# Other byte offsets for weights, h and turned output, and a later place for the split of the turned output

## The chip, the cores and the metric

The kernel runs on one core of one Trainium2 chip. The metric is the device time of one execution in microseconds (us). A profile of one execution gives, for each engine, what ran when and what it waited for. The engines are PE (TensorE, matrix products; the loads of its stationary operand are listed as PEld), ACT (ScalarE), DVE (VectorE), POOL (GpSimd) and SP (the engine that issues most of the transfers). Working memory (SBUF) has 128 partitions; a byte offset in this text is the offset within one partition. Products land in the PSUM banks.

## What is computed

With x of 2048 rows and 576 columns, everything in float32:

```
xn  = layernorm(x)
q, k, v = split(xn @ wqkv)            # 32 heads of 18 columns
logits[s, w] = q[s] . k[s - 2 w] / sqrt(18),  w = 0..7   (masked where s - 2 w < 0)
o   = sum_w softmax(logits)[s, w] * v[s - 2 w]
h   = relu(xn @ w1)                   # 4608 columns
out = x + o @ wo + h @ w2
```

## The kernel before

**Precision.** PE multiplies in the type float32r. Each operand that needs the full precision is split into a high part (ACT copies it to float32r) and a low part (DVE subtracts the high part from the raw value). A product is then three: high by high, high by low, low by high. `hi_lo` (L278) makes such a pair of operations.

**Work and order.** The 2048 rows are handled in two phases (`NPH`) of 1024 rows (8 row tiles, each of 128 rows). In a phase there are 18 blocks `n` of 256 columns of w1, and for each block two halves `h` of 512 rows; such a pair is a group `g`, 72 in all. A group makes h for its block (first layer, x moving and a *weight set* `wset` stationary, 256 columns at a time), splits h into `hhi` and `hlo`, and multiplies them by `w2t` (second layer, `o_step`, L720: h stationary, w2 moving in pieces of 256 and 320 columns; six matmuls, three products by two pieces, make one step, and a step writes the accumulator `po`). Most groups form the first layer by seven products of sums (`pstep`, L605, called P1 to P7) in place of eight plain ones (`classic`, L583). For one block in about four, q, k and v of a quarter of the heads are made too (`qkv_tile`, L778; x stationary, 432 columns of wqkv moving, 14 matmuls, 8 tiles per quarter and phase, 64 in all), and the attention of that quarter follows on DVE (`attention`, L818).

**The turned output.** The output of attention must be stationary for the product with wo, so it has to be turned. DVE turns it in blocks of 32 by 32 (`turn`, L881), SP stores it to DRAM as `turned` (L891), and `wo_h` (L666) loads it back in column order into `olo` (L681, or L685 for the 16 leftover columns of each quarter), lets ACT copy the high part to `ohi` and lets DVE subtract to leave the low part in `olo`. Steps of kind "wo" in `o_step` then use `ohi` and `olo` as stationary operands, with `v` (a buffer of the pool vp, here holding wo, split by `wo_make`, L519) moving.

**What sets the order.** The program is written out by a planner (`Order`, L53). PE's order is given by the loops. ACT and DVE each have a list of waiting operations; an operation becomes ready when the planner thinks its predecessors have ended, and among the ready ones the one with the earliest due time goes first. Work of attention on DVE goes into a background list (`later`) that fills the gaps. A transfer (`send`, L151) is issued on SP in the order of the calls; its assumed landing time is worked out from its size, and a `margin` can be added to it (L160):

```
        op.end = max(start + 2.1, self.dma + 1.2) + margin
```

On the chip each engine runs its instructions in the written order and each waits for its own semaphores. The margin is thus not a wait; it only changes where the planner places what depends on the transfer.

**Where tiles lie.** Tiles lie one behind the other, in the order of the pools and, within `keep`, of the calls. `keep` holds x (`X`), its split and summed forms (`XA`, `XS`, `XR`), the two weight sets (`BUF`; set 0 for even blocks, set 1 for odd ones, and for wqkv in the block before), k (`KK`), `TS`, q/o (`QO`) and two sums. Then come `w2p` (w2), `hp` (h), `whp` (the turned output), `vp` (v and wo), and the rest.

Of the kernel before, what the change touches and what calls it, by code (L numbers as in the profile page):

```python
# [16 lines left out]
P = 128  # L17
# [11 lines left out]
WOP = ((6, 9, 13, 16), (7, 10, 14, 17))  # L29
HALO = ((0, 112), (112, 127))  # L30
WARM = 24

S2, S4, S3, S1 = range(4)
T1, B11, T2, B21, T3, B22, T4, RR = range(8)
# [155 lines left out]
def tile_body(ctx: ExitStack, tc: tile.TileContext, x, wqkv, wo, w1, w2, out):  # L190
# [14 lines left out]
    ctx.enter_context(tc.manual_schedule())  # L205
    pool = lambda name, bufs, **k: ctx.enter_context(tc.tile_pool(name=name, bufs=bufs, **k))
    keep = pool("keep", 1)
    w2p = pool("w2p", 4)
    hp = pool("hp", 5)
    whp = pool("whp", 2)  # L210
    vp = pool("vp", 2)
    prp = pool("prp", 2)
    lgp = pool("lgp", 1)
    smp = pool("smp", 2)
    mvp = pool("mvp", 8)
    dram = pool("dram", 1, space=bass.MemoryType.DRAM)
    psp = pool("psp", 1, space=PSUM)

# [11 lines left out]
    XA = [[keep.tile([P, 2, KT, TBN], F32R, name=f"xa{h}{j}") for j in range(2)] for h in range(2)]  # L230
    XS = [keep.tile([P, 2, 4, 2, TBN], F32R, name=f"xs{h}") for h in range(2)]
    XR = [keep.tile([P, 3, TBN], F32R, name=f"xr{h}") for h in range(2)]
    BUF = [keep.tile([P, 10 * 3 * UD], F32R, name=f"wset{b}") for b in range(2)]
    KK = keep.tile([P, W - 1 + NI, UD], F32, name="kk")
    TS = keep.tile([P, 4, 2, P], F32, name="ts")
    VV = {}
# [7 lines left out]
    bk3 = psp.tile([P, 512], F32, name="bk3")  # L244
    pm = psp.tile([P, 512], F32, name="pm")

    def wset(m):
        z = BUF[m % 2].rearrange("p (e c) -> p e c", e=2)[:, :, 0:2048]
        return z.rearrange("p e (s k c) -> p e s k c", s=8, k=2)

    def wqset(p):
        return BUF[(p + 1) % 2].rearrange("p (t c) -> p t c", t=10)

    def raw_view(z):
        v = z.rearrange("p w c -> p (w c)")[:, 0 : 8 * TBN].rearrange("p (j s k c) -> p j s k c", j=2, s=2, k=2)
        return [v[:, 0], v[:, 1]]
# [18 lines left out]
    def mm(o, l, r, start, stop):  # L275
        nc.tensor.matmul(o, l, r, start=start, stop=stop, skip_group_check=True)  # L276

    def hi_lo(hi, lo, raw, n, after, slack):  # L278

        a = act(lambda: copy(hi, raw), n, after, slack)  # L280
        b = dve(lambda: sub(lo, raw, f32(hi)), n, [a], slack + 0.8)
        return [a, b]
# [215 lines left out]
    def wq_make(p, u, kts, raw=None):  # L498

        w = wqset(p)  # L500
        b = (p + 1) % 2
        v = wqkv.rearrange("r (s c) -> r s c", s=3)[:, :, u * UD : (u + 1) * UD] if raw is not None else WQC[u]
        for kt in kts:
            z = raw[:, kt] if raw is not None else f32(w)[:, 5 + kt]
            after = [] if raw is not None else [kept["wq", u]]
            free = slots_free(b, range(432 * kt // 256, min(7, (432 * kt + 431) // 256) + 1))
            if raw is None:
                after += free
            z3 = z.rearrange("p (s c) -> p s c", s=3)
            if kt < KT:  # L510
                g = [send(lambda: nc.sync.dma_start(z3, v[kt * P : (kt + 1) * P]), 221, after)]
            else:
                g = [send(lambda rows=rows: nc.sync.dma_start(z3[rows], v[KT * P : D]), 110, after)
                     for rows in (slice(0, DR), slice(DR, P))]
            WQOK.setdefault(p, []).extend(hi_lo(w[:, kt], w[:, 5 + kt], z, 3 * UD, [*g, *free], 2.5))

    WO, WOOK = {}, {}

# [147 lines left out]
    def wo_h(g, u, j):  # L666
        ph, n, h = G[g]
        i = 4 * h + 2 * j
        if g == NG - 1:
            z = w2p.tile([P, 2, D], F32R, name="w2t")  # L670
            ni = 4
            hi, lo = z[:, 0, 0 : ni * P], z[:, 1, 0 : ni * P]
            for q in range(2):
                WOH[g, u, q] = hi[:, q * TBN : (q + 1) * TBN], lo[:, q * TBN : (q + 1) * TBN]
        else:
            ni = 2
            hi, lo = whp.tile([P, TBN], F32R, name="ohi"), whp.tile([P, TBN], F32R, name="olo")
            WOH[g, u, j] = hi, lo
        v = lambda z: z.rearrange("p (i c) -> p i c", i=ni)
        if u < NU:  # L680
            s = [send(lambda: nc.sync.dma_start(v(f32(lo)), OT[u, i : i + ni].rearrange("i c k -> c i k")), 128, turned[ph, u])]  # L681
            low = lambda: sub(lo, f32(lo), f32(hi))
        else:
            s = [
                send(lambda rows=rows: nc.sync.dma_start(v(f32(lo)[rows]), OTR[i : i + ni].rearrange("i c k -> c i k")), 64, turned[ph, u])  # L685
                for rows in (slice(0, DR), slice(DR, P))
            ]
            low = lambda: sub(hi[DR:P], f32(lo[DR:P]), f32(hi[DR:P]))
        a = act(lambda: copy(hi, f32(lo)), ni * P, s, 4)
# [88 lines left out]
    def qkv_tile(p, u, i):  # L778
        ph = p // NP
        if i == 0:  # L780
            o_.force(KFREE[0])
            VV[u % 2] = vp.tile([P, W - 1 + NI, UD], F32, name="v")
            nc.gpsimd.memset(KK[0:1, 0 : W - 1, :], 0.0)
            nc.gpsimd.memset(VV[u % 2][0:1, 0 : W - 1, :], 0.0)
        k, v, q = KK, VV[u % 2], QO[u % 2]
        h, j, c = place(i)
        xa, wq = XA[h][j], wqset(p)
        o = pm[:, 0 : 3 * UD]
        lst = (
            [(xa[:, 0, kt, c], kt) for kt in range(KT)] + [(xa[:, 1, kt, c], kt) for kt in range(KT)]  # L790
            + [(XR[h][:, j, c], 4)] + [(xa[:, 0, kt, c], 5 + kt) for kt in range(KT)] + [(XR[h][:, j, c], 9)]
        )

        def f():
            for z, (l, b) in enumerate(lst):
                mm(o, l, wq[:, b], z == 0, z == len(lst) - 1)

        t = pe(f, 14 * 0.196, [*WQOK[p], *XOK[h, j], *BANK["pm"]])
        pq = o.rearrange("p (s c) -> p s c", s=3)

        def out_():
            copy(k[:, W - 1 + i, :], pq[:, 1])
            copy(v[:, W - 1 + i, :], pq[:, 2])
            copy(q[:, i, :], pq[:, 0])

        e = act(out_, 3 * (UD + 70), [t, *OFREE[u % 2]], 1.2)
        BANK["pm"] = [e]
        SETFREE[(p + 1) % 2] = {q: t for q in range(8)}
# [9 lines left out]
    def attention(ph, u, halo):  # L818
# [4 lines left out]

        def begin():
            s["lg"] = lgp.tile([P, NI, W, HG], F32, name="lg")
            s["m"] = smp.tile([P, NI, HG], F32, name="m")
            s["r"] = smp.tile([P, NI, HG], F32, name="r")

        def spread(z):
            return z[:, :, None, :].to_broadcast([P, NI, W, HG])  # L830
# [208 lines left out]
        RAWR.pop(h, None)  # L1039

    def x_home(h):
        KR[h] = raw_view(vp.tile([P, W - 1 + NI, UD], F32, name="v") if h else KK)

    for h in range(2):
        g = GP - 1 + h
# [32 lines left out]

    x_first(0)
    x_first(1, nc.scalar)  # L1080
    VV[0] = vp.tile([P, W - 1 + NI, UD], F32, name="v")
    ST0 = VV[0].rearrange("p w c -> p (w c)")[:, 0:1280].rearrange("p (s k c) -> p s k c", s=5, k=2)
    RAWS = ((B11, 0, 0), (B21, 256, 0), (RR, 512, 0), (B12, 0, 1), (B22, 256, 1))
    SETOK[0] = {}
# [24 lines left out]

    KFREE[0] = WQOK[0]  # L1110
    OFREE[0] = [*W2OK[0, 0], *W2OK[0, 1]]
    KR[0] = raw_view(vp.tile([P, W - 1 + NI, UD], F32, name="v"))
# [127 lines left out]
```

## Time and profile before

| | |
|---|---|
| median of 3 runs | 1200.48 us (1198.25 to 1200.82) |
| the profiled execution | 1201.66 us |
| its span, first to last instruction | 1199.9 us |
| granted TensorE clock, mean | 0.990 |
| DMA, mean | 96 GB/s |

The profile comes as a page (busy shares, slices, DMA, the chain, the costliest groups, the transfers), and its trace answers further questions. In rows of groups, `out<-in` names what is written and read, then come partitions and elements, the count, the busy time in us with the mean of one in ns, and behind the second bar the idle time before, with what ended it. A matmul's duration overlaps the next one's, so the pace is the distance of the starts, not the duration. The chain is the work that ended last, followed back from the end. Rows of waits read "engine, line, waited for, engine, line: us in total, times, longest us". Rows of the timeline and of the chain begin with the start and the length in us.

### The profile page before, as it was taken

Reading aid. Unit: us, or ns where it says so; the run is one execution under the profiler, and the core shown is the slowest. Engines: PE = TensorE matmul, PEld = TensorE weight load, DVE = VectorE, ACT = ScalarE, POOL = GpSimd, SP = SyncE. Lnnn points to the kernel's source line nnn. Section 1 sums busy time; section 2 is a strip of 40 time slices with the busy share of each in tenths; the row PEclk is TensorE's granted clock in tenths of the full one; section 3 lists DMA queues with packets and bytes.
Section 4 is the critical chain, followed back from the end, with each engine's and each line's share of the span. In section 5 each row is a group of like instructions: output and inputs, shape, how many; then the busy total and the mean of one; then the engine's idle time right before and its main releaser. Section 6 shows DMA issues by size and latency. Waiting matters only on the chain.

```text
span 1199.9 us, 21930 instructions
## 1 busy us (share of the span) xinstructions
PE 1162.5 (97%) x8528; PEld 1140.0 (95%) x8528; DVE 826.4 (69%) x1533; ACT 743.0 (62%) x1658; POOL 64.2 (5%) x97
## 2 busy tenths in 40 slices
PE   7999999999988999999999999999999999999998
PEld 6899999999988999899999999999999999999998
DVE  7648978953988169774683299589925994399731
ACT  5548466655656466566686567476646665566663
POOL 2200200110011001000010000000000000000000
PEclk8999999999999999899999999999999999999999
DMA  6752441562245232333352222231322213221322
GB/s 197 218 139 69 150 106 56 161 170 84 68 148 158 42 92 83 120 78 88 120 173 93 71 66 58 44 103 44 89 54 85 71 52 72 83 59 56 80 66 89
DMA packets 133544, 115.60 MB, mean 96 GB/s; under 512 B 54128, under 2 KB 112240, under 8 KB 133120
## 3 DMA queue, kind: packets, MB, share of 16 engines
q1 hardware_dynamic: 128192, 85.00, 25.7%
q0 software_dynamic: 5104, 28.90, 7.5%
q8 instruction: 67, 1.10, 0.4%
q14 instruction: 37, 0.30, 0.1%
q10 hardware_dynamic: 144, 0.29, 0.1%
HBM read 96.01 MB, written 36.50 MB: 110 GB/s over the span
## 4 chain that ended last, share of the span: by engine, by line
PE 73%; DVE 12%; ACT 8%; issue 3%; DMA 3%; POOL 0%; SPq 0%; ACTq 0%; DVEq 0%; POOLq 0%
PE po L276 32%; PE bk L276 21%; PE pm L276 14%; PE bkA L276 5%; DVE wset L273 3%; ACT po L270 2%; ACT x L270 2%; DVE ts L273 2%; DMA olo<-turned 1%; DVE hlo L554 1%; ACT wset L270 1%; DVE sn L273 1%; ACT hhi L270 1%; DVE pr L870 1%; DVE pr L840 1%
## 5 line engine op out<-in xcount | busy, mean ns | idle before, releaser
L276 PE MATMUL po<-w2t,hhi 128*128 128x256 f32 (+1 forms) x2304 | 407.1, 299 | 6.1 <-ACT po L270 5.9
L276 PEld LDWEIGHTS po<-w2t,hhi 128*128 128x128 f32 x2304 | 341.0, 190 | 10.9 <-ACT po L270 9.7
L276 PE MATMUL po<-w2t,hlo 128*128 128x256 f32 (+1 forms) x1152 | 248.1, 297 | 0.0
L276 PE MATMUL bk<-xs,wset 128*128 128x256 f32 x1632 | 238.2, 282 | 7.0 <-DVE sn L273 7.0
L270 ACT ACTIVATE x<-po 128x576 f32<-128x576 f32 x286 | 182.2, 644 | 100.3 <-PE po L276 97.6
L276 PEld LDWEIGHTS bk<-xs,wset 128*128 128x128 f32 x1632 | 217.7, 189 | 8.1 <-DVE sn L273 7.8
L276 PEld LDWEIGHTS po<-w2t,hlo 128*128 128x128 f32 x1152 | 195.7, 191 | 0.0
L270 ACT ACTIVATE po<-x 128x576 f32<-128x576 f32 x286 | 187.0, 654 | 2.9
L276 PE MATMUL pm<-wset,xa 128*128 128x432 f32 x768 | 172.9, 360 | 2.6 <-ACT wset L270 1.5
L276 PEld LDWEIGHTS pm<-wset,xa 128*128 128x128 f32 x768 | 140.2, 188 | 9.9 <-ACT qo L270 2.3
L276 PE MATMUL bk<-xa,wset 128*128 128x256 f32 x924 | 138.7, 288 | 7.5 <-DVE hlo L554 4.8
L273 DVE TENSOR_TENSOR sn<-bk,sn 128x256 f32<-128x256 f32 x136 | 57.2, 421 | 122.0 <-PE bk L276 81.2
L276 PEld LDWEIGHTS bk<-xa,wset 128*128 128x128 f32 x924 | 125.8, 193 | 13.2 <-DVE hlo L554 10.1
L273 DVE TENSOR_TENSOR w2t<-w2t 128x576 fp32r<-128x576 f32 (+1 forms) x72 | 54.1, 751 | 70.1 <-ACT w2t L270 69.4
L270 ACT ACTIVATE hhi<-sn 128x256 fp32r<-128x256 f32 x136 | 56.4, 415 | 72.7 <-DVE sn L273 72.7
L270 ACT ACTIVATE kk<-pm 128x144 f32<-128x144 f32 (+1 forms) x68 | 21.0, 308 | 114.6 <-PE pm L276 114.4
L870 DVE TENSOR_TENSOR pr<-lg,v 128x1152 f32<-128x1152 f32 x64 | 85.1, 1352 | 0.2
L276 PE MATMUL bk<-xr,wset 128*128 128x256 f32 x426 | 85.1, 281 | 0.0
L840 DVE TENSOR_TENSOR pr<-qo,kk 128x1152 f32<-128x1152 f32 x64 | 85.0, 1351 | 0.0
L843 DVE TENSOR_REDUCE lg<-pr 128x64 f32<-128x1152 f32 x64 | 84.8, 1345 | 0.0
L273 DVE TENSOR_TENSOR wset<-wset 128x512 fp32r<-128x512 f32 (+2 forms) x120 | 70.8, 599 | 11.9 <-ACT wset L270 11.5
L276 PE MATMUL bkA<-xa,wset 128*128 128x256 f32 x480 | 68.9, 281 | 2.0 <-DVE xr L273 2.0
(132 smaller groups left out, 1365.5 us busy)
## 6 DMA issues: line engine op xcount, KB each, us to landing
w2t<-w2c SPq DMA_DIRECT2D x70, 288.0 KB, 2.8
wset<-w1c SPq DMA_DIRECT2D x106, 128.0 KB, 2.4
w1c<-in_w POOLq DMA_DIRECT2D x18, 576.0 KB, 8.4
w2c<-in_w POOLq DMA_DIRECT2D x18, 576.0 KB, 8.8
wset<-wqc SPq DMA_DIRECT2D x28, 216.0 KB, 2.5
out<-x SPq DMA_DIRECT2D x16, 288.0 KB, 2.2
wset<-w1c SPq DMA_DIRECT2D x70, 64.0 KB, 2.2
ts<-w1c SPq DMA_DIRECT2D x34, 128.0 KB, 2.7
```

The lines of the kernel that those rows point to most:

```text
L270: nc.scalar.activation(o, i, func)
L273: nc.vector.tensor_tensor(o, a, b, op=op)
L276: nc.tensor.matmul(o, l, r, start=start, stop=stop, skip_group_check=True)
L554: nc.vector.scalar_tensor_tensor(lo, src, 0.0, f32(hi), op0=ALU.max, op1=ALU.subtract)
L840: nc.vector.tensor_tensor(pr[i], q, window(k, i), op=ALU.mult)
L843: nc.vector.tensor_reduce(s["lg"][:, i], pr.pop(i).rearrange(heads, d=Dh), axis=AX.X, op=ALU.add)
L870: nc.vector.tensor_tensor(pr[i].rearrange(heads, d=Dh), e, window(v, i).rearrange(heads, d=Dh), op=ALU.mult)
```

## The change

It has two parts.

*Addresses.* Three pads are put between pools and one into `keep`. The weight sets get 2 x 2176 columns each in place of 4320, so that the high half and the low half lie a whole number of 256 bytes apart, and `wqset` takes five row blocks from either half. The buffers of vp get 2176 columns, too. To make room, the pool of small statistics goes from 8 to 6 buffers, and m and r of the softmax from 2 to 1. From the sizes follow the offsets modulo 256 bytes:

| tile | before | after |
|---|---|---|
| x forms xa, xs, xr | 192 | 192 |
| weight set 0, high and low half | 192, 128 | 0, 0 |
| weight set 1, high and low half | 64, 0 | 0, 0 |
| w2t, high and low half | 128, 128 | 0, 0 |
| hhi, hlo | 128 | 128 |
| ohi, olo | 128 | 128 |
| v / wo, its two buffers | 128, 64 | 0, 0 |
| kk | 192 | 0 |
| ts, qo, sn | 128 | 192 |

h and the turned output move by whole multiples of 256 bytes; against the operands that they are multiplied with, they change.

*Order.* The load of the turned output gets a margin of 2.5 us (1.5 us for the leftover columns), so the planner places the copy to `ohi` and the subtraction to `olo` behind other work. PE's order and POOL's order stay as they are. On ACT and DVE the copies and subtractions move by a few places, and other operations shift with them. On SP six loads of a weight set move behind the stores of the turned output and the load of the leftover columns, once near the end of each phase.

```
@@
+PADS = (16, 16, 32, 32)
@@
     keep = pool("keep", 1)
+    pad1 = pool("pad1", 1).tile([P, PADS[1]], F32, name="pad1")
     w2p = pool("w2p", 4)
+    pad2 = pool("pad2", 1).tile([P, PADS[2]], F32, name="pad2")
     hp = pool("hp", 5)
     whp = pool("whp", 2)
+    pad3 = pool("pad3", 1).tile([P, PADS[3]], F32, name="pad3")
     vp = pool("vp", 2)
...
-    mvp = pool("mvp", 8)
+    mvp = pool("mvp", 6)
@@
-    BUF = [keep.tile([P, 10 * 3 * UD], F32R, name=f"wset{b}") for b in range(2)]
+    keep.tile([P, PADS[0]], F32, name="pad0")
+    BUF = [keep.tile([P, 2, 2176], F32R, name=f"wset{b}") for b in range(2)]
@@
+    def v_tile():
+        return vp.tile([P, 2176], F32, name="v")[:, 0 : (W - 1 + NI) * UD].rearrange("p (w c) -> p w c", w=W - 1 + NI)
+
     def wset(m):
-        z = BUF[m % 2].rearrange("p (e c) -> p e c", e=2)[:, :, 0:2048]
+        z = BUF[m % 2][:, :, 0:2048]
         return z.rearrange("p e (s k c) -> p e s k c", s=8, k=2)
 
     def wqset(p):
-        return BUF[(p + 1) % 2].rearrange("p (t c) -> p t c", t=10)
+        return BUF[(p + 1) % 2][:, :, 0 : 5 * 3 * UD].rearrange("p e (t c) -> p e t c", t=5)
@@ wq_make
-            z = raw[:, kt] if raw is not None else f32(w)[:, 5 + kt]
+            z = raw[:, kt] if raw is not None else f32(w)[:, 1, kt]
...
-            WQOK.setdefault(p, []).extend(hi_lo(w[:, kt], w[:, 5 + kt], z, 3 * UD, [*g, *free], 2.5))
+            WQOK.setdefault(p, []).extend(hi_lo(w[:, 0, kt], w[:, 1, kt], z, 3 * UD, [*g, *free], 2.5))
@@ wo_h
-            s = [send(lambda: nc.sync.dma_start(v(f32(lo)), OT[u, i : i + ni].rearrange("i c k -> c i k")), 128, turned[ph, u])]
+            s = [send(lambda: nc.sync.dma_start(v(f32(lo)), OT[u, i : i + ni].rearrange("i c k -> c i k")), 128, turned[ph, u], 2.5)]
...
-                send(lambda rows=rows: nc.sync.dma_start(v(f32(lo)[rows]), OTR[i : i + ni].rearrange("i c k -> c i k")), 64, turned[ph, u])
+                send(lambda rows=rows: nc.sync.dma_start(v(f32(lo)[rows]), OTR[i : i + ni].rearrange("i c k -> c i k")), 64, turned[ph, u], 1.5)
@@ attention
-            s["m"] = smp.tile([P, NI, HG], F32, name="m")
-            s["r"] = smp.tile([P, NI, HG], F32, name="r")
+            s["m"] = smp.tile([P, NI, HG], F32, name="m", bufs=1)
+            s["r"] = smp.tile([P, NI, HG], F32, name="r", bufs=1)
```

`qkv_tile` takes its row blocks by two indices in place of one, and the other places that took a buffer named v from vp call `v_tile`; both do the same as before.

More of the change, by code (lines that the diff above doesn't have):

```diff
@@ L781, in qkv_tile @@
             o_.force(KFREE[0])
-            VV[u % 2] = vp.tile([P, W - 1 + NI, UD], F32, name="v")
+            VV[u % 2] = v_tile()
             nc.gpsimd.memset(KK[0:1, 0 : W - 1, :], 0.0)
@@ L789, in qkv_tile @@
         lst = (
-            [(xa[:, 0, kt, c], kt) for kt in range(KT)] + [(xa[:, 1, kt, c], kt) for kt in range(KT)]
-            + [(XR[h][:, j, c], 4)] + [(xa[:, 0, kt, c], 5 + kt) for kt in range(KT)] + [(XR[h][:, j, c], 9)]
+            [(xa[:, 0, kt, c], (0, kt)) for kt in range(KT)] + [(xa[:, 1, kt, c], (0, kt)) for kt in range(KT)]
+            + [(XR[h][:, j, c], (0, 4))] + [(xa[:, 0, kt, c], (1, kt)) for kt in range(KT)] + [(XR[h][:, j, c], (1, 4))]
         )
@@ L795, in f @@
             for z, (l, b) in enumerate(lst):
-                mm(o, l, wq[:, b], z == 0, z == len(lst) - 1)
+                mm(o, l, wq[:, b[0], b[1]], z == 0, z == len(lst) - 1)
         t = pe(f, 14 * 0.196, [*WQOK[p], *XOK[h, j], *BANK["pm"]])
@@ L1041, in x_home @@
     def x_home(h):
-        KR[h] = raw_view(vp.tile([P, W - 1 + NI, UD], F32, name="v") if h else KK)
+        KR[h] = raw_view(v_tile() if h else KK)
     for h in range(2):
@@ L1080, in tile_body @@
     x_first(1, nc.scalar)
-    VV[0] = vp.tile([P, W - 1 + NI, UD], F32, name="v")
+    VV[0] = v_tile()
     ST0 = VV[0].rearrange("p w c -> p (w c)")[:, 0:1280].rearrange("p (s k c) -> p s k c", s=5, k=2)
@@ L1111, in tile_body @@
     OFREE[0] = [*W2OK[0, 0], *W2OK[0, 1]]
-    KR[0] = raw_view(vp.tile([P, W - 1 + NI, UD], F32, name="v"))
+    KR[0] = raw_view(v_tile())
     KR[1] = [
```

## The prediction

> **What bounds the kernel now.** I read the page first: the busy shares, the chain, the groups.
>
> ```profile
> span 1199.9 us, 21930 instructions
> PE 1162.5 (97%) x8528; PEld 1140.0 (95%) x8528; DVE 826.4 (69%) x1533; ACT 743.0 (62%) x1658; POOL 64.2 (5%) x97
> PE 73%; DVE 12%; ACT 8%; issue 3%; DMA 3%; POOL 0%; SPq 0%; ACTq 0%; DVEq 0%; POOLq 0%
> ```
>
> TensorE is busy for 97% of the span and holds 73% of the chain that ends last. So two things can move the time: how fast 8528 matmuls follow one another, and the few microseconds in which PE waits. The change touches both: the addresses touch the first, the later split touches the second. Next came the groups with shapes kept apart, for the counts.
>
> ```profile
> L276 PE MATMUL po<-w2t,hhi 128*128 128x320 f32 x1152 | 335.1, 313 | 0.0
> L276 PE MATMUL bk<-xs,wset 128*128 128x256 f32 x1632 | 238.2, 282 | 7.0 <-DVE sn L273 7.0
> L276 PE MATMUL po<-w2t,hlo 128*128 128x320 f32 x576 | 179.8, 312 | 0.0
> L276 PE MATMUL bk<-xa,wset 128*128 128x256 f32 x924 | 138.7, 288 | 7.5 <-DVE hlo L554 4.8 <-ACT xa L270 2.0
> L276 PE MATMUL bkA<-xa,wset 128*128 128x256 f32 x480 | 68.9, 281 | 2.0 <-DVE xr L273 2.0
> ```
>
> The second layer (w2t moving, h stationary) is 1152 + 576 = 1728 pairs of one matmul of 256 and one of 320 columns. The first layer (x moving, a weight set stationary) is 1632 + 924 + 480 = 3036 matmuls of 256 columns, in sixes, beside the short rest rows. Matmuls overlap, so their pace is read from the starts of successive groups in the timeline.
>
> **The stalls that the later split aims at.** Of the waits in two windows, the olo transfer comes first in both, followed by DVE behind ACT, and then PE itself.
>
> ```profile
> ACT ohi L270 <- DMA olo<-turned: 5.5, 1, 5.5
> DVE olo L273 <- ACT ohi L270: 4.1, 1, 4.1
> PE bk L276 <- DVE sn L273: 2.7, 1, 2.7
> PEld po L276 <- ACT po L270: 0.7, 1, 0.7
> ```
>
> ```profile
> ACT ohi L270 <- DMA olo<-turned: 5.6, 1, 5.6
> DVE olo L273 <- ACT ohi L270: 4.2, 1, 4.2
> PE bk L276 <- DVE sn L273: 2.9, 1, 2.9
> ```
>
> The first fence is 340 to 370 us, the second 478 to 510 us. The chain says how 5.5 us of ACT become 2.7 us of PE:
>
> ```profile
> 342.93 8.22 DMA olo<-turned
> 351.17 0.42 ACT ohi L270
> 351.62 0.42 DVE olo L273
> ...
> 353.65 0.35 DVE sn L273
> ```
>
> The transfer of the turned output takes 8.22 us here, where the median for these transfers is 2.7 us:
>
> ```profile
> olo<-turned SPq DMA_DIRECT2D x30, 128.0 KB, 2.7
> ```
>
> ACT stands before its copy, DVE stands before the subtraction that needs the copy, and behind that subtraction in DVE's queue is the sum sn, which frees the bank that PE's next product writes.
>
> **What the 2.5 us do.** They are no wait on the chip: they are added to the landing time that the planner assumes, so only the written order changes. In the changed program ohi stands one place later on ACT at this spot (behind the first hhi<-sn), and olo stands behind sn on DVE, where before it stood ahead of it. So sn no longer waits for the transfer, and the 2.7 and 2.9 us of PE go: -5.6 us. What is late next is ACT: it still stops at ohi until 351.17, with the second hhi<-sn, an evacuation of po and a fresh seed of po behind it. PE waits for such a seed already (the 0.7 us row), and it now reaches that point sooner; I give back 0.6 us, about that row, over both places: **-5.0 us**. Bounds: nothing gained, if ACT's stop replaces DVE's in full; 7.0 us gained, if the 0.7 us and as much at the second place go too. The four instructions that overtake cost nothing; ohi and olo get later by about 1 us and are first used ten microseconds after this landing:
>
> ```profile
> 361.33 0.70 PE L276 MATMUL po<-v,ohi 128*128 128x256 f32 x4
> ```
>
> If that cover were gone, one subtraction of 0.42 us would be seen in each place. On the weights of the next set, too, the order shifts: at the end of each phase the six loads of a weight set now queue on SP behind four stores of turned, one store and one load of the 16 leftover columns, where before they stood ahead of these.
>
> ```profile
> 526.37 0.58 SPq L902 DMA_DIRECT2D o<-qo  x1
> 527.39 2.28 SPq L891 DMA_DIRECT2D turned<-pr  x4
> 529.77 0.58 SPq L906 DMA_DIRECT2D pr<-o  x1
> 534.67 0.61 ACT L270 ACTIVATE wset<-wset 128x512 fp32r<-128x512 f32 x1
> ...
> 539.11 0.37 ACT L270 ACTIVATE bkA<-bk 128x256 f32<-128x256 f32 x1 [0.75 <-PE bk L276]
> 547.98 1.90 PE bk L276 x16
> ```
>
> From the first of these to the end of the last is 4.0 us, so the loads go out by about that much later. The four splits on ACT that ended at 535.3 now stand behind the bkA copy of 539.11 and would end near 542 (four by 0.61 us). PE turns to that set no sooner than 547.98, so it costs nothing, with some 6 us to spare; without the cover it would be up to 4.0 us, once in each phase. The smaller pools (mv from 8 to 6 buffers, m and r from 2 to 1) only tie an operation to the one six rows, or one attention block, before it. A block's m and r are dead before the next block begins, and the normalisations of the second phase are spread over many groups: nothing, and if a statistic did wait for a buffer, DVE is free for 31% of the span.
>
> **What the addresses do.** From the tile sizes, in the order of allocation: x (xa, xs, xr) begins at 192 modulo 256 bytes before and after. A weight set's high and low halves lie at 192 and 128 (even sets), 64 and 0 (odd sets); after, at 0 and 0 in both. w2t goes from 128 to 0, h stays at 128. While one matmul streams, the next stationary operand is loaded, so I look at that one's offset less the moving one's: second layer 0 before, 128 after; first layer 0 and -64, or 128 and 64, before, always 64 after. QKV's row blocks step by 192 through all offsets before and after; the first two rows are odd sets, the third is an even one:
>
> ```profile
> 1004.66 2.74 PE pm L276 x14
> 872.80 2.76 PE pm L276 x14
> 134.01 2.73 PE pm L276 x14
> ```
>
> They differ by 0.01 to 0.03 us a tile, and after, both kinds start at 0: over the 32 tiles of the odd sets that is at most 1 us either way, taken as nothing.
>
> Does the offset matter at all? The output projection gives one like-for-like pair: v is moving and ohi stationary at 128, while v lies at 128 in one buffer and at 64 in the other. The first row below is the buffer at 128 (960 to 999 us), the second the one at 64 (1089 to 1127 us):
>
> ```profile
> L276 PE MATMUL po<-v,ohi 128*128 128x320 f32 x16 | 4.6, 311 | 0.0
> L276 PE MATMUL po<-v,ohi 128*128 128x320 f32 x16 | 4.6, 309 | 0.0
> ```
>
> So 64 apart is 2 ns quicker than 0 apart per 320 columns. For the first layer, an even set and an odd set, each six followed by the group that begins when it hands over:
>
> ```profile
> 1042.82 0.87 PE L276 MATMUL bk<-xs,wset 128*128 128x256 f32 x6
> 1043.52 0.40 PE L276 MATMUL bk<-xr,wset 128*128 128x256 f32 x2
> ...
> 1063.21 0.88 PE L276 MATMUL bk<-xs,wset 128*128 128x256 f32 x6
> 1063.93 0.69 PE L276 MATMUL po<-w2t,hhi 128*128 128x256 f32 x4
> ```
>
> The even six takes 0.70 us, the odd one 0.72 us: 2 to 3 ns per matmul between the offsets, so the pace does hang on them, by about 2%. Second layer: 128 apart is not in its trace. The nearest row is its own shape, 64 apart, 2 ns less per pair; the other bound is the odd sets, whose high half is 128 apart and 0.02 us per six (3.3 ns per matmul) slower than the even ones. I take the nearest row: 1728 x 2 ns = **-3.5 us**; ends -7 us (4 ns, as if both matmuls of a pair gained like the one in the row) and 2 x 1728 x 3.3 ns = +11 us. First layer: after, all 506 sixes are 64 apart, which only an odd set's low half has now; between all like even (253 x 0.02 = -5 us) and all like odd (+5 us) I take **0**.
>
> [...]
>
> **Sum.** -5.0 - 3.5 + 0 = -8.5 us. The profiled execution took 1201.66 us, that is 1.76 us around its span of 1199.9, and lies 1.2 us above the median of 1200.48 us; against itself it comes to 1193.2, and in terms of the median to **1192 us**. Three runs lie between 1198.25 and 1200.82, so 0.2% (2.4 us) is about what can be told from no change.
>
> **Rivals.**
> - *128 apart collides.* If the second layer runs as the odd sets do against the even ones, it loses up to 11 us, and with the stalls gone the time is 1200.5 - 5 + 11 = 1206.5 us; it decides for slower from a loss of 7.4 us, 2.1 ns per matmul. For it: 0.72 against 0.70 us. Against it: in the same sets the low half is 64 apart, and the slow part may be that. 24%.
> - *Every layer gains.* If 64 apart gives the first layer the even sets' 0.70 throughout and the second 4 ns per pair, it is -5 - 5 - 7 = -17: 1183 us. For it: the gain of the 320-column row goes the same way. 18%.
> [...]
> - *The order changes nothing.* ACT keeps ohi ahead of hhi<-sn and of the seeds until the transfer lands, so that PE stops there instead; with little from the addresses this gives 1198 to 1203 us. For it: ACT's 5.5 us stay. Against it: the chain passes through DVE's sn, which is freed. 10%.
> - The forecast, 1187 to 1197 us: 36%.
>
> **How the numbers follow.** Faster: 36 + 18 + 12% = 66%. Same: 10%, the order's rival. Slower: 24%. The range reaches from 1178, past the second rival, to 1205, most of the first: about 15% lie outside. For the forecast alone it is 1187 to 1197.
>
> **What would show it.** In the waits of the two windows, PE behind sn and DVE olo behind ACT ohi should be gone, and ACT behind the olo transfer still there, shorter or not. Two pairs of w2t matmuls should start about 2 ns closer each, so the x1152 row's 313 ns should read 311 or less; sixes of the first layer should read the same, near 0.71 us, in even and odd sets. The prediction is wrong if the 320-column row rises to 315 or more, if the sixes leave 0.70 to 0.72, or if a wait of PE on wset, ohi or po of over 3 us turns up.

## The result, and the profile after

The changed kernel takes 1187.1 us (median of four runs, 1186.3 to 1188.1) where the kernel before takes 1200.65 us: ratio 0.989, 95% interval 0.9872 to 0.9907. Run again later beside other kernels it stood at 0.9871 (0.9854 to 0.9889). The forecast was 1192 us: the sign and the range held, the gain was 13.5 us where 8.5 were forecast. 1187.1 us lies at the very edge of the forecast's own 1187 to 1197 us, nearer to the rival *every layer gains* (1183 us) than to 1192.

The first lines of the page after, with the line of the chain:

```profile
span 1184.6 us, 21915 instructions
PE 1142.5 (96%) x8528; PEld 1115.6 (94%) x8528; DVE 824.2 (70%) x1533; ACT 742.4 (63%) x1658; POOL 64.4 (5%) x97
PE 64%; DVE 20%; ACT 6%; issue 4%; DMA 4%; SPq 0%; POOL 0%; DVEq 0%; ACTq 0%; POOLq 0%
```

TensorE is busy for 20.0 us less with the same 8528 matmuls, yet the span is only 15.3 us shorter. DVE's share of the chain rose from 12 to 20%: matmuls became quicker and wait more. The groups, shapes kept apart, show both (busy us, mean ns of one, then idle time before and who ended it):

```profile
L284 PE MATMUL po<-w2t,hhi 128*128 128x320 f32 x1152 | 326.1, 305 | 0.0
L284 PE MATMUL po<-w2t,hhi 128*128 128x256 f32 x1152 | 317.5, 285 | 10.1 <-ACT po L278 9.9
L284 PE MATMUL bk<-xs,wset 128*128 128x256 f32 x1632 | 232.9, 278 | 2.2 <-DVE sn L281 2.2
L284 PE MATMUL po<-w2t,hlo 128*128 128x320 f32 x576 | 175.5, 305 | 0.0
L284 PE MATMUL bk<-xa,wset 128*128 128x256 f32 x924 | 136.1, 285 | 12.5 <-DVE hlo L562 9.1 <-ACT xa L278 3.3
```

The 320-column rows fell from 313 and 312 to 305 ns, the xs row of the first layer from 282 to 278. PE behind sn fell from 7.0 to 2.2 us, but PE behind hlo rose from 4.8 to 9.1. The waits of the two windows, 330 to 360 and 468 to 498 us (us in total, times, longest):

```profile
ACT ohi L278 <- DMA olo<-turned: 4.3, 1, 4.3
PEld po L284 <- ACT po L278: 2.8, 5, 1.3
DVE olo L281 <- ACT ohi L278: 2.2, 1, 2.2
PE po L284 <- ACT po L278: 1.8, 3, 1.1
```

```profile
ACT ohi L278 <- DMA olo<-turned: 4.9, 1, 4.9
DVE olo L281 <- ACT ohi L278: 2.9, 1, 2.9
PEld po L284 <- ACT po L278: 2.8, 3, 2.0
PE po L284 <- ACT po L278: 2.1, 2, 1.8
```

PE behind sn is gone from both. ACT still stands before the transfer, and now PE stands behind ACT's seeds of po. The forecast had not looked at the granted clock in these places. The view by stretches (busy us of each engine, then PEclk, DMA share, GB/s), first before, then after:

```profile
350.00:360.00 10.00, 6.80 (x39) 6.27 (x38) 8.38 (x15) 4.09 (x10) 0.00 (x0) 0.83 0.22 62
390.00:400.00 10.00, 10.00 (x57) 9.86 (x58) 1.53 (x4) 5.17 (x13) 0.00 (x0) 0.83 0.40 66
490.00:500.00 10.00, 7.15 (x36) 6.95 (x35) 9.16 (x16) 4.39 (x10) 0.00 (x0) 0.66 0.19 54
```

```profile
340.00:350.00 10.00, 9.73 (x78) 9.37 (x77) 7.70 (x14) 4.97 (x11) 0.00 (x0) 1.00 0.75 252
380.00:390.00 10.00, 8.71 (x58) 8.17 (x59) 5.21 (x15) 7.62 (x19) 0.00 (x0) 1.00 0.57 112
480.00:490.00 10.00, 7.89 (x62) 7.46 (x62) 7.43 (x14) 4.35 (x10) 0.00 (x0) 1.00 0.28 79
```

Before, a clock of 0.83 and 0.66 follows the two stops, and another 0.83 follows stops that PE makes at 384 to 389 us, not behind olo; in this execution of the changed kernel it stays at 1.00 in all three places. 0.17 and 0.34 of 10 us are 1.7 and 3.4 us of clock: 5.1 us behind the two stops, 1.7 us at the third place. The third place can't be put down to the change. The changed kernel traced a second time (e5 below) has the low clock there again:

```profile
380.00:390.00 10.00, 8.32 (x48) 8.05 (x49) 5.68 (x15) 7.80 (x17) 0.00 (x0) 0.83 0.62 119
```

Of the other runs below, e1, e6, e10 and e11 have it there too, and e2, e3, e4 and e8 don't.

The records of the granted clock in the trace before give half the full clock for 3.41 us from 356.0 us, for 3.41 us from 390.1 us and for 6.83 us from 492.5 us, that is for one window of 3.41 us or two. In this trace stops of 2.7 and 2.9 us came before the windows at 356.0 and 492.5 us; in the 3.41 us ahead of 356.0, 390.1 and 492.5 us TensorE stood for 1.94, 2.20 and 2.10 us (from a matmul's recorded end to the next start), and the last section sets the other traces beside these.

Since TensorE runs the same matmuls in the same order in every version, the starts of the same matmul in two traces can be subtracted. That gives where the time went (us, one profiled execution each, against the kernel before; e1 and e2 are the experiments below):

```
matmuls       at (us)     before   after  addresses(e1)  order(e2)
   0- 120      1-  31      29.2    +0.7       -0.2         +0.8
 120-2400     31- 350     319.7    -3.1       -3.6          0.0
2400-2760    350- 410      60.0    -5.7       +0.3         -5.2
2760-3240    410- 475      65.1    -0.8       -0.7          0.0
3240-3480    475- 512      36.9    -3.7       +0.2         -2.1
3480-4080    512- 590      77.3    +0.1       -1.1         +0.5
4080-4320    590- 622      32.3    +1.1       -0.5         +1.3
4320-5400    622- 777     154.8    -1.4       -1.3          0.0
5400-5520    777- 793      16.0    +1.0        0.0         +1.1
5520-8280    793-1163     369.8    -4.8       -4.4         -0.3
8280-end    1163-1196      33.2    +1.4       -0.5         +1.7
```

The gain has two kinds: a slow, steady one wherever TensorE simply runs, and two steps where the stops were. And there are three places with a loss that the forecast did not have. Each column is one execution: the second trace of the changed kernel (e5) differs from the first by up to 1.4 us in a row, at 350 to 410 us, where its low clock is back, and at 777 to 793 us it loses 0.2 us in place of 1.0.

### The profile page after: what moved, and what is told of

It reads as the page before. It is cut to its first block, busy times and chain, and to the rows that moved or that the text cites. A ratio compares the mean times of both kernels' runs of the same rounds, so it can differ in the third digit from the quotient of the medians.

```text
span 1184.6 us, 21915 instructions
## 1 busy us (share of the span) xinstructions
PE 1142.5 (96%) x8528; PEld 1115.6 (94%) x8528; DVE 824.2 (70%) x1533; ACT 742.4 (63%) x1658; POOL 64.4 (5%) x97
## 4 chain that ended last, share of the span: by engine, by line
PE 64%; DVE 20%; ACT 6%; issue 4%; DMA 4%; SPq 0%; POOL 0%; DVEq 0%; ACTq 0%; POOLq 0%
PE po L284 26%; PE bk L284 18%; PE pm L284 14%; PE bkA L284 5%; DVE wset L281 4%; DVE pr L885 3%; DVE hlo L562 2%; DVE ts L281 2%; DVE pr L878 2%; DMA olo<-turned 1%; DVE sn L281 1%; ACT x L278 1%; ACT po L278 1%; ACT wset L278 1%; DMA wset<-wqc 1%
## 5 line engine op out<-in xcount | busy, mean ns | idle before, releaser
L284 PE MATMUL po<-w2t,hhi 128*128 128x256 f32 (+1 forms) x2304 | 399.9, 295 | 10.1 <-ACT po L278 9.9
L284 PEld LDWEIGHTS po<-w2t,hhi 128*128 128x128 f32 x2304 | 332.5, 188 | 18.1 <-ACT po L278 16.4
L284 PE MATMUL po<-w2t,hlo 128*128 128x256 f32 (+1 forms) x1152 | 244.2, 293 | 0.0
L284 PE MATMUL bk<-xs,wset 128*128 128x256 f32 x1632 | 232.9, 278 | 2.2 <-DVE sn L281 2.2
L284 PEld LDWEIGHTS bk<-xs,wset 128*128 128x128 f32 x1632 | 212.2, 188 | 3.0 <-DVE sn L281 2.6
L284 PEld LDWEIGHTS po<-w2t,hlo 128*128 128x128 f32 x1152 | 190.4, 188 | 0.0
L284 PE MATMUL bk<-xa,wset 128*128 128x256 f32 x924 | 136.1, 285 | 12.5 <-DVE hlo L562 9.1
L284 PEld LDWEIGHTS bk<-xa,wset 128*128 128x128 f32 x924 | 123.0, 192 | 18.8 <-DVE hlo L562 14.6
L562 DVE SCALAR_TENSOR_TENSOR hlo<-bk,hhi 128x256 fp32r<-128x256 f32 x77 | 32.2, 418 | 57.1 <-ACT hhi L278 57.0
```

The costliest lines, as they stand in the source:

```text
L562: nc.vector.scalar_tensor_tensor(lo, src, 0.0, f32(hi), op0=ALU.max, op1=ALU.subtract)
```

## The experiments

**e1: the addresses alone**, and **e2: the order alone.**

```
e1, against the changed kernel
-  ... 128, turned[ph, u], 2.5)]          ... 64, turned[ph, u], 1.5)
+  ... 128, turned[ph, u])]               ... 64, turned[ph, u])
e2, against the kernel before
-  ... 128, turned[ph, u])]               ... 64, turned[ph, u])
+  ... 128, turned[ph, u], 2.5)]          ... 64, turned[ph, u], 1.5)
```

> The changed kernel with both margins taken back (2.5 and 1.5 to 0): the new addresses alone. Theory A (addresses quicken the matmuls of both layers, and the later split by itself takes away the two stops of 2.7 and 2.9 us together with the lower clock behind them): the matmuls gain about 12 us, the two stops stay, so 1188 to 1193 us; rows of 320 columns near 305 ns as in the changed kernel, first layer near 278 to 285 ns; PE behind sn still 2.5 to 3 us in each of the two places and the granted clock below 0.9 right behind them. Rival B (addresses don't matter, all 13.5 us come from the order): 1199 to 1202 us. Rival C (the order brought nothing, all comes from the addresses): 1186 to 1188 us.

> The kernel before with the two margins (2.5 and 1.5 us) alone: the new order at the old addresses. Theory A: the stops of PE behind sn go, and with them the slices of clock 0.83 and 0.66 behind them: 1192 to 1196 us (the recorded forecast has 1195.5 for the order alone, without any term for the clock). Rival C (ACT's stop takes the place of DVE's): 1198 to 1203 us. Rival B (all from the order): 1186 to 1189 us. Rows of 320 columns stay at 311 to 313 ns by A and C.

Measured, beside the kernel before at 1202.28 us: the addresses alone 1189.07 us, ratio 0.9893 (0.9881 to 0.9906), so some 12.9 us; the order alone 1197.6 us, ratio 0.9965 (0.9953 to 0.9977), so some 4.2 us. Rival B, that all comes from the order, falls. The order's 1197.6 us lies between theory A (1192 to 1196 us) and rival C (1198 to 1203 us): the part below shows that each holds for a share. In e1 the rows are as quick as in the changed kernel, in e2 they are not (e1, then e2):

```profile
L284 PE MATMUL po<-w2t,hhi 128*128 128x320 f32 x1152 | 327.8, 306 | 0.0
L276 PE MATMUL po<-w2t,hhi 128*128 128x320 f32 x1152 | 333.5, 312 | 0.0
```

In e1 the stops have not gone but grown, from 2.7 and 2.9 to 4.7 and 3.8 us (e1, waits of PE in 340 to 370 and 470 to 505 us, one line of each, then the stretch with the first stop):

```profile
PE bk L284 <- DVE sn L281: 4.7, 1, 4.7
```

```profile
PE bk L284 <- DVE sn L281: 3.8, 1, 3.8
```

```profile
345.00:355.00 10.00, 5.27 (x33) 5.08 (x32) 5.26 (x12) 3.55 (x8) 0.00 (x0) 0.84 0.31 89
```

Quicker matmuls come sooner to a transfer that is late anyway, so that part of their gain is waited away: in e1 PE came to the first stop 3.8 us sooner than before, while the copy behind the transfer began only 1.9 us sooner, at 349.3 in place of 351.2 us. In e2 PE's waits in these two windows are all for seeds of po (waits of PE, first and second window), the first stretch runs at full clock, and the second still has one window at half clock (1.7 us):

```profile
PE po L276 <- ACT po L270: 1.7, 2, 1.4
```

```profile
PE po L276 <- ACT po L270: 1.9, 3, 1.3
```

```profile
345.00:355.00 10.00, 8.58 (x67) 8.26 (x66) 7.15 (x13) 4.40 (x11) 0.00 (x0) 1.00 0.66 223
490.00:500.00 10.00, 10.00 (x69) 10.00 (x68) 9.68 (x18) 4.83 (x10) 0.00 (x0) 0.83 0.02 6
```

The table says what makes up e2's net gain in this execution: 5.2 and 2.1 us won in the two places, 1.3, 1.1 and 1.7 us lost in the three others. Of the 5.2 us, 1.7 are the clock of the third place, which e5, with the same new order, has lost again.

**e3 and e4: each layer's address change undone.**

```
e3   -PADS = (16, 16, 32, 32)        w2t from 0 to 128, h stays at 128
     +PADS = (16, 48, 0, 32)         (and without the tile pad2)
e4   -BUF = [keep.tile([P, 2, 2176], F32R, ...) for b in range(2)]
     +BUF = [keep.tile([P, 10 * 3 * UD], F32R, ...) for b in range(2)]
     (pad0 behind it; the weight sets at 192, 128 and 64, 0 again)
```

> The changed kernel with w2t back at offset 128 modulo 256 (h stays at 128), all else as changed: the second layer's part undone. Theory A (the second layer's gain is its own addresses'): the row of 320 columns goes back from 305 to 312 or 313 ns, the first layer stays at 278 to 285, and 1728 pairs lose about 5 ns each, 9 us, of which some lies in waits: 1192 to 1196 us. If the pace of the second layer is set by something else (the first layer's weights, the order): 1186 to 1189 us and 305 ns.

> The changed kernel with the weight sets back at their old offsets (192 and 128, 64 and 0; w2t 0, h 128 and the order as changed): the first layer's part undone. Theory A: the first layer's matmuls of 256 columns go back from about 115 to 118 ns apart, 3 ns for some 3600 of them, 11 us, of which some lies in waits: 1193 to 1199 us, and w2t's row of 320 columns stays at 305 ns. If the first layer's offsets do nothing, as the prediction had it: 1186 to 1189 us.

Measured: e3 1195.25 us, ratio 0.9953 (0.9939 to 0.9967); e4 1193.23 us, ratio 0.9925 (0.9913 to 0.9937). Both times lie where theory A had them, but not for its reason. The rows of e3 and then e4:

```profile
L283 PE MATMUL po<-w2t,hhi 128*128 128x320 f32 x1152 | 333.3, 312 | 0.0
L283 PE MATMUL bk<-xs,wset 128*128 128x256 f32 x1632 | 236.0, 281 | 2.1 <-DVE sn L280 2.1
```

```profile
L284 PE MATMUL po<-w2t,hhi 128*128 128x320 f32 x1152 | 328.9, 308 | 0.0
L284 PE MATMUL bk<-xs,wset 128*128 128x256 f32 x1632 | 237.2, 281 | 1.3 <-DVE sn L281 1.3
```

In e3 only w2t was moved, and the untouched first layer slowed as well, from 278 to 281 ns. In e4 only the weight sets were moved, and the untouched second layer went from 305 to 308. The timeline shows it at one spot, first of the changed kernel, then of e3 (start, length, group; a six runs from its start to that of the next row):

```profile
927.83 0.68 PE L284 MATMUL po<-w2t,hhi 128*128 128x256 f32 x4
928.35 0.42 PE L284 MATMUL po<-w2t,hlo 128*128 128x256 f32 x2
928.61 0.85 PE L284 MATMUL bk<-xa,wset 128*128 128x256 f32 x6
929.30 0.39 PE L284 MATMUL bk<-xr,wset 128*128 128x256 f32 x2
```

```profile
934.01 0.70 PE L283 MATMUL po<-w2t,hhi 128*128 128x256 f32 x4
934.54 0.43 PE L283 MATMUL po<-w2t,hlo 128*128 128x256 f32 x2
934.80 0.87 PE L283 MATMUL bk<-xa,wset 128*128 128x256 f32 x6
935.51 0.40 PE L283 MATMUL bk<-xr,wset 128*128 128x256 f32 x2
```

The three pairs take 0.78 us in the one and 0.79 in the other, the six 0.69 and 0.71 us. Over the whole program the mean distance between starts (distances above 135, 165 and 212 ns for 256, 320 and 432 columns, and above 80 ns for the few of 128, left out as stops) was:

```
before 133.27   order alone 133.26   w2t back (e3) 132.67   weight sets back (e4) 132.50
addresses alone 130.83   changed 130.83 ns
```

So one layer's new offsets alone bring 0.6 or 0.8 ns per matmul, both together 2.4 ns. They do not add up: what one layer does depends on the other. 2.44 ns for 8200 matmuls are 20 us, of which some 13 reach the end in e1. Theory A, each layer for itself, falls, and with it the way in which the prediction reckoned with addresses: layer by layer, offset pair by offset pair. In e3 and e4 kk, ts, qo, sn and v keep their new offsets; what these bring by themselves no run shows.

**e5 and e6: the changed kernel again, and the margin at two projections only.**

```
-  ... turned[ph, u], 2.5)]                                  ... turned[ph, u], 1.5)
+  ... turned[ph, u], 2.5 if ph == 0 and u in (1, 2) else 0.0)]   ... turned[ph, u])
```

> The changed kernel itself, beside the next one on one chip. Its ratio to the kernel before was 0.989 (0.9872 to 0.9907) and that of the addresses alone 0.9893 (0.9881 to 0.9906). If order and addresses add up (0.9965 and 0.9893), it should stand at 0.986, 1185 us against 1202; if the places in which the later split costs time eat what it saves, at 0.988 to 0.990 again.

> The changed kernel with the margin of 2.5 us kept only for the second and third output projection of the first phase (the two places with the stops of 2.7 and 2.9 us), and 0 everywhere else. Matmul by matmul, the kernels with the new order gained 9 us against the old order in three stretches (350 to 390 and 475 to 512 us) and lost 1.0, 1.0 and 1.4 us in three others (590 to 622, 777 to 793 and the last 32 us). Theory A (the losses come from the margin at the other projections): those three stretches go back to the pace of the kernel with the addresses alone, the two stops stay away, so 3 to 4 us less than the changed kernel, ratio 0.985 to 0.987. Rival (the losses come from the earlier arrival, whatever the margin there): no difference, 0.988 to 0.990.

Measured: e5 1186.69 us, 0.9871 (0.9854 to 0.9889); e6 1184.3 us, 0.9854 (0.9836 to 0.9871). Whether the two parts add up (0.9858) or not can't be told from e5. The totals of e5 and e6 overlap, but stretch by stretch e6 answers: the last 33 us went from +1.4 (e5) to -0.3, so this loss was the margin's, and it stays away in e10 and e11 below, which have no margin there either (-0.5 and -0.3). At 590 to 622 us e6 has 0.0 where e5 has +0.9, but e10 and e11, with e6's written order there, have +0.4 and +1.1 again, and 777 us stays between +0.2 and +1.0 in all of them: what sets these two is open, beyond that e1, with the old order, has neither. e6 also won less at 475 to 512 us (-1.3 against -4.3). That is not the margin: by the traces ACT, DVE and SP have the same written order in e5 and e6 from 253 to 553 us, and e8 below, with e6's order throughout, has -4.3 there. e6's execution has a window at half clock behind its stop there (1.7 us from 487.7 us on), and e5's has none. A single trace thus says little about 1 to 3 us in a stretch with a stop.

**e7: bare matmuls** (one execution). The core of the kernel, with `mm` one matmul between slices at chosen offsets:

```
for pre in ((128, 128), (0, 128)):
    for mo in OFF:
        for so in OFF:
            pairs(*pre, 8); six(mo, so, 48)
for pre in ((192, 192), (192, 0)):
    for mo in OFF:
        for so in OFF:
            six(*pre, 16); pairs(mo, so, 24)
...
```

> Leaves out the whole computation: matmuls alone, on zeros, with no other engine at work. Streams of 48 matmuls of 256 columns, and of 24 pairs of 256 and 320 columns, for all 16 pairs of offsets (moving, stationary) modulo 256 bytes, each after two different preludes; then five times eight matmuls of the first layer's kind (moving at 192) and six pairs (stationary at 128) for all 16 pairs of offsets of weight set and w2t. Theory D (one pair of offsets sets one pace): each pair of offsets gives one distance between starts whatever came before it; 192 and 0 give 114 ns, 0 and 128 give 120 and 140 ns, 128 and 128 give 117 and 149 ns, also in the mixed stretches. Theory E (a pattern that carries over from matmul to matmul): the same pair of offsets gives different distances after different preludes, or in the mixed stretches, as the changed kernel with one layer's offsets taken back showed (118 in place of 114 ns in the untouched first layer). Theory F (the pace comes from the other engines' accesses): all 16 pairs run alike here.

All tiles came to lie 128 bytes further on than written, which keeps every distance; the offsets below are the true ones. Two streams of the same matmuls (moving at 64, stationary at 128, the distance of the changed first layer) after the two preludes, as the timeline has them (42 matmuls each; window from the ninth matmul of the stream on):

```profile
110.19 5.11 PE L36 MATMUL b<-mv,st 128*128 128x256 f32 x42
```

```profile
234.21 4.92 PE L36 MATMUL b<-mv,st 128*128 128x256 f32 x42
```

117.8 ns from start to start after the one prelude and 113.3 after the other, held through the stream, with no other engine at work. The streams settle near a few values: 113.3, 117.8, 118.7 and 120.0 ns for 256 columns; 260.0, 263.4 and 266.7 ns for a pair. Theory F falls (the pace isn't due to other engines), and so does D (one pair of offsets, one pace). E stands as far as this goes: the pace differs with the offsets, and at the same offsets with what ran before (117.8 or 113.3 ns). One kind of pair did go with one pace: where both operands have the same offset modulo 256 bytes, all 16 streams (four offsets, two shapes, two preludes) ran at the slowest pace, 120.0 or 266.7 ns. Before the change w2t and h stood so, and x against the high half of the even sets.

**e8 and e9: the offsets of e7's best mixture in the kernel, and the table in the kernel's own mixture.**

```
e8, against e6:  -PADS = (16, 16, 32, 32)     x 192, weight sets 128, w2t 192, h 128, v 192
                 +PADS = (0, 16, 48, 16)      (kk allocated ahead of the weight sets, no pad0)
e9   for ho in OFF:
         for so in OFF:
             for mo in OFF:
                 for _ in range(4):
                     six(192, so, 8); pairs(mo, ho, 3); six(192, so, 6); pairs(mo, ho, 6)
```

> The kernel with the margin in two places only, and other offsets: x 192, weight sets 128, w2t 192, h 128, v 192 (the stationary operand always 64 bytes below the moving one, modulo 256). In the table of bare matmuls the mixed stretch with these distances ran at 123.35 ns per matmul, the changed kernel's distances at 124.34, the old ones at 125.6 to 127.4. Theory E (the pace is set by the offsets of the whole sequence, and the bare table carries over): rows of the first layer near 113.5 ns apart, pairs near 260 ns, 1.0 ns less for some 8000 matmuls, 8 us, of which a third to a half goes into waits for DVE and ACT: 1178 to 1181 us against 1184 to 1187. Rival (the kernel's other sequences spoil it, or the waits take all of it): 1183 to 1187 us.

> Leaves out the whole computation: bare matmuls on zeros in the kernel's own mixture (8 of 256 columns, 3 pairs, 6 of 256, 6 pairs, four times over), x moving at 192 throughout, for all 64 triples of offsets of weight set, w2t and h modulo 256. By theory E the triples 0, 0, 128 (the changed kernel) and 128, 192, 128 lie at 123 to 125 ns per matmul, 128 or 0 with w2t 128 and h 128 (the old one) at 126 to 127.5; and shifting h and w2t together by 64 changes the result, because what the one layer leaves behind decides the pattern in which the other starts. If only the distance within each layer counts, triples with equal distances run alike.

e8 missed: 1192.21 us, ratio 0.9924 (0.9903 to 0.9945), slower than e6 by about 8 us where 3 to 6 were to be won. e9 (one execution) says why. Four of its 64 triples (weight set, w2t, h): 0, 0, 128, which is the changed kernel; 128, 192, 128, which is e8; 0, 128, 128, which is e3; 192, 128, 128, like an even set's high half before. The timeline has 98 matmuls of each:

```profile
534.07 12.24 PE L37 MATMUL b<-mv,st 128*128 128x256 f32 x98
...
711.02 12.49 PE L37 MATMUL b<-mv,st 128*128 128x256 f32 x98
...
565.93 12.55 PE L37 MATMUL b<-mv,st 128*128 128x256 f32 x98
...
759.43 12.59 PE L37 MATMUL b<-mv,st 128*128 128x256 f32 x98
```

From start to start these are 122.95, 125.42, 126.03 and 126.45 ns. The changed kernel's triple is the quickest of all 64 (122.95 to 127.27), and the 16 with w2t and h at one offset all lie above 125.5. Moving w2t and h on together, with the weight sets at 0, gives 122.95, 124.62, 124.63 and 123.09 ns, so the distance within a layer isn't enough either. For e8's triple e9 has 117.6 ns in the first layer and 117.9 + 145.8 in a pair; in the kernel e8 had 117.7 and 117.75 + 145.8. e7 had measured the same distances, all 128 bytes further on and in another mixture, at 123.35. The four triples come in the order of their kernels (130.83, 132.41, 132.67 and 133.27 ns over the whole program, measured as above), so the table of bare matmuls that had the kernel's sequence and offsets carried over to the kernel in order.

**e10 and e11: margins by place.**

```
e10  -  ... turned[ph, u], 2.5)]                        +  ... 2.5 if u < NU - 1 else 0.0)]
e11                                +  ... (7.0 if ph == 0 and u else 2.5) if u < NU - 1 else 0.0)]
     (both: 0 in place of 1.5 at the leftover columns)
```

> The changed kernel with the margin of 2.5 us at the first three output projections of each phase and 0 at the last of each phase and at its leftover columns. Matmul by matmul it should keep what the changed kernel gains at 350 to 390 and 475 to 512 us (8 to 9 us against the addresses alone) and lose nothing at 590 to 622 us and in the last 32 us, where the changed kernel lost 1.0 and 1.4 us: 1184 to 1185 us, ratio 0.985 to 0.987. If it stands where the changed kernel stands (0.987 to 0.990), those two stretches were no loss of the margin.

> As the kernel before it, but 7.0 us in place of 2.5 at the second and third output projection of the first phase. There ACT stood before the late olo transfer for 4.2 to 5.7 us with the seeds of po behind its copy ohi, and PE waited 1.6 to 3.2 us for those seeds; with 7.0 us two seeds of po and both splits of sn stand ahead of ohi on ACT. Theory G (ACT's stop took the place of DVE's, as the recorded rival said, for part of the gain): PE's waits for the seeds fall below 1 us in both windows and the time falls by another 2 to 4 us, clock dips included: 1181 to 1183 us. Rival (ohi comes too late for its product, or the stop moves on to DVE or to the weight loads of the next group): 1185 us or more, with PE behind ohi or olo.

Measured, beside 1200.96 us: e10 1184.01 us, 0.9859 (0.9839 to 0.9878), as expected in total, though it won only 2.4 us at 350 to 410 us, where the changed kernel, with the same written order there, won 5.7 and 4.3: PE stood 2.2 us behind seeds of po, and a window at half clock followed. e11 took 1179.73 us, 0.9822 (0.9805 to 0.9838), below the 1181 to 1183 us expected, the quickest of all kernels here and 7 us below the changed one. Of e11's waits in 330 to 372 us these two are all that PE has, where the changed kernel had 1.8 us:

```profile
PE po L284 <- DVE olo L281: 0.4, 1, 0.4
PE po L284 <- ACT po L278: 0.3, 1, 0.3
```

Where the two stops were, its stretches run without one and at full clock:

```profile
345.00:355.00 10.00, 10.00 (x82) 10.00 (x82) 10.00 (x20) 5.95 (x13) 0.00 (x0) 1.00 0.26 80
480.00:490.00 10.00, 10.00 (x85) 10.00 (x84) 9.96 (x20) 6.46 (x15) 0.00 (x0) 1.00 0.24 69
```

Theory G holds: with ohi written behind the seeds on ACT, the stop is gone from PE; what is left is 0.3 us behind the seeds in each window, and 0.4 and 0.6 us behind olo. In the stretch at 475 to 512 us e11 is 6.0 us below the kernel before, the changed kernel 3.7.

## Why the prediction was right, and where it was not

*Stalls, -5.0.* The order alone brought 4.2 us (2.8 to 5.6), so the size held, but by luck: what the working left out on either side about cancels. The 2.7 and 2.9 us of PE behind sn went, as written. Three terms were missing or too small. First, the low clock behind the two stops, 5.1 us of clock in two slices, which the profile before shows and the forecast never priced; the changed kernel has none of it in either trace, e2 kept 1.7 us. (The 1.7 us at 390 us can't be counted for the change: e5 loses them again.) Second, "what is late next is ACT", given back at 0.6 us: PE's waits for the seeds are 1.8 and 2.1 us in the two windows of the changed kernel. e11, which takes ACT's stop away too, is worth 4.3 us against e10. The recorded rival "the order changes nothing" thus had its mechanism right for a part, and its size wrong. Third, the new order loses 1.1, 1.0 and 1.4 us at 590, 777 and 1163 us (0.9, 0.2 and 1.4 us in e5), the last of them by the margin of the last projection, as e6, e10 and e11 show; no step of the prediction looked at these places, since in the trace before no stop of over 0.4 us stood there.

*Second layer, -3.5, and first layer, 0.* These are the terms that were mis-sized: the addresses alone bring 12.9 us. From start to start a pair went from 266.6 to 261.4 ns, 9.0 us for the 1728 pairs where 3.5 were priced, and a matmul of the first layer from 118.0 to 114.9 ns, some 9.5 us for 3036 where nothing was; a part of both is waited away. The step that failed is the pricing of one offset pair by its nearest row, each layer for itself. The rows were real, but each pace belonged to a sequence, not to a pair of offsets, as e3, e4, e7 (113.3 or 117.8 ns at one pair) and e9 show. That a stationary operand is loaded while matmuls run, from which the prediction set its offset against the moving one's, the profile before does show: PE is busy for 1162.5 us and PEld for 1140.0 us of a span of 1199.9 us, so both at once for at least 1102.6 us. The distance of 64, "which only an odd set's low half has now", stood in the slower sixes, the odd ones at 0.72 us; in the changed kernel, at 64 throughout, a six is the quickest of the three, 0.69 us where the even sets had 0.70. The rival "every layer gains" had the sign right in both layers at 1183 us, though it was priced pair by pair too; "128 apart collides" reasoned in the same pairwise way and went the wrong way.

*Addresses don't matter.* That nothing but the stalls go, 12% of the recorded chances, means 1200.5 less 5.0 us, 1195.5 us. e1, with the addresses alone, is 12.9 us below the kernel before, and the bare matmuls of e7 stand 113.3 to 120.0 ns apart for the same 256 columns, by their offsets and what ran before. Both decide against it.

*Queues and pools.* The later loads behind the turned stores cost nothing that a trace shows: in the changed kernel no wait of PE stands in 515 to 545 us. The smaller pools bring no wait of PE that e2, with the larger ones, lacks.

*What would show it.* The x1152 row fell below 311 ns, PE behind sn left both windows and ACT behind olo stayed, as written. DVE olo behind ACT ohi, which should have gone too, did not: 2.2 and 2.9 us are left of 4.1 and 4.2. The sixes left 0.70 to 0.72 downwards, which the prediction had named as a sign of its error, and it was one.

*The way to the end.* TensorE lost 20 us of busy time and the span 15.3: PE's waits for sn, hlo and po together went from 18.1 to 21.6 us, although sn's went down by 4.8. That the quicker pace makes these waits is seen in e1, where only addresses changed and the same three come to 23.4 us.

## What to carry to other kernels

A margin in a planner is worth giving place by place: behind a late transfer move everything that others wait for ahead of the consumer, on each engine that stops, and leave the rest alone (e11 took 1179.73 us, e5, with the margin everywhere, 1186.69 us). Price a stop of TensorE with the low clock that may follow it (here 1.7 us behind the stop of 2.7 us and 3.4 us behind that of 2.9 us), not by its own length alone. Offsets of matmul operands were worth 12.9 of 1202.28 us here, a per cent, but only a measurement in the kernel's own sequence and at its own offsets told so: pairs of offsets forecast 3.5 us, and the table in another mixture forecast 1178 to 1181 us for e8, which took 1192.21. The one pair that these runs advise against is the same offset modulo 256 bytes for both operands (120.0 and 266.7 ns in e7, its slowest paces).

## What was not expected of the hardware

- In e7 the pace of back-to-back matmuls of one shape takes a few values (113.3 to 120.0 ns for 256 columns, 260.0 to 266.7 for a pair of 256 and 320) and holds the one that it settles on; the same offsets ran at 113.3 or 117.8 ns. What in the chip makes the pattern is not settled by these runs.
- Of two layers that take turns, a change of the one's offsets slowed the other's untouched matmuls (278 to 281 ns in e3, 305 to 308 ns in e4).
- The half clock came in windows of 3.413 us, on a grid that stays fixed within a run: before, they begin at 356.0, 390.1 and 492.5 us, 10 and 30 windows apart. Cut along this grid, from 60 to 1160 us of the 11 traces of full kernels, the traces give the time that TensorE stands in each window (from a matmul's recorded end to the next start). All 14 windows after which the clock fell had 1.58 us or more of it; of some 3500 after which it stayed full, only three had more than that (1.62, 1.69 and 1.74 us). In these traces, then, the half clock began only behind 1.58 us of standing or more in one window, so where a stop fell on the grid counted beside its length. A stop of 2.1 us (from start to start) in the changed kernel lay across two windows, with 1.30 and 0.81 us of standing, and nothing followed; one of 2.1 us in e10 lay in a single window, with 1.81 us, and a window at half clock followed. A second such window came three times, where TensorE stood for 0.75 us or more within the first, and never where it stood for 0.48 us or less.
